# Spreading the first chunk's decays with one single-pass product over 128 stacked rows, and two blocks-of-four of warm-up instead of eleven blocks

## The chip, the cores and the metric

The kernel runs on one core of a Trainium2 chip. The metric is the device time of one execution in microseconds (us). An execution has a span, from its first to its last instruction, and some time around it. The engines are TensorE (PE, its weight loads shown apart as PEld), VectorE (DVE), ScalarE (ACT), GpSimd (POOL) and SyncE (SP), which here only issues DMAs.

## What is computed

A chunked state-space scan (4 batches, 8 heads, 768 positions) is followed by a gated feed-forward layer. Cut to what matters:

```python
for c in range(nc):                                  # chunks of the sequence
    cum = np.cumsum(log_a[:, :, sl], axis=-1)        # log_a = log(clip(a, 1e-6, 1))
    L = np.exp(cum[:, :, :, None] - cum[:, :, None, :]) * causal
    M = np.einsum('bhin,bhjn->bhij', Cc, Bc) * L     # scores times decays
    y[:, :, sl] = einsum(M, xc) + einsum(Cc, state) * exp(cum)
    state = exp(sum(la)) * state + sum(B x, decayed to the chunk's end)
out = (sigmoid(y @ w_gate) * (y @ w_val)) @ w_out    # 3072 tokens, 256 -> 1536 -> 256
```

The kernel never takes a logarithm: the decays L are running products of `a`, made by a multiplying scan.

## The kernel before

The sequence is cut into six chunks of 128 positions, each worked as two halves of 64 (`L2`). The feed-forward layer of a chunk follows once its scan is done, so TensorE has a long, dense middle, and a start in which the first chunk must go through the scan before there is anything to multiply with the weights. The first chunk is worked in four units, one for each batch (class `FirstUnit`), in the order 0, 3, 1, 2.

A planner (`run`) emits every instruction in an order that is fixed by a table of numbers (`DUES`); each engine then executes its own list strictly in that order and waits where a semaphore tells it to. So an early step of an engine that waits for a DMA holds everything behind it on that engine.

What the change touches is the path from the raw `a` to the decays of the first chunk:

- `a0` is the first chunk's `a`, 64 rows (`R2`; half of the chunk, batch, head) of 64 positions, loaded by SP's first DMA.
- `ac` is `a0` clipped, with its first column set to zero (DVE).
- `apart` holds, for each of the 64 rows, its values in the block of 64 columns that belongs to its head, and zeros elsewhere: `ac` times `head2`, a 0/1 selector (DVE). Its lower 64 partitions are filled with zeros by POOL.
- `of_unit[:, b]` is a 0/1 matrix that picks batch b's rows, and repeats them over the 64 partitions of each half. The product of it with `apart` (PE, `spread`, L741, tile `pa`, 128x512, in float32) puts each row's `a` on all partitions that need it.
- The DVE scan at L744 turns `pa` into the decays `dec` (tile `ab`). There are four such products and four such scans, one for each unit.
- Before all that TensorE multiplies a tile of zeros (`warm`, L237): eleven blocks of 128 columns in three instructions, `WARM = (4, 4, 3)`.

Around this path, in the same lists, stand `products` (the transposes `pt` of B and C, L756 and L757, and the score products `pcb`, L691), `result` (DVE's `weigh` L695, which multiplies scores and decays into the tile `m`; then TensorE's L706 and L716), and `split_w`, which cuts a block of weights (tile `wr`) into parts in five steps: DVE L482, ACT L488, DVE L490, ACT L495, POOL L497. The first of them is the split of the first gate block; in DVE's list its step L482 stands ahead of the first scan.

Two waits of DVE's and PE's lists are not plain from the code. The banks of PSUM for `pt`, `pa` and the small product `pp` are three, used in turn: the third `pa` waits for the first scan to read the first `pa`, the fourth for the second scan. And the first `m` waits for the third scan, which stands just ahead of it on DVE.

Of the kernel before, what the change touches and what calls it, by code (L numbers as in the profile page):

```python
# [8 lines left out]
F32 = mybir.dt.float32  # L9
F32R = mybir.dt.float32r  # L10
# [3 lines left out]
ALU = mybir.AluOpType  # L14
# [121 lines left out]
}  # L136
WARM = (4, 4, 3)
PE0 = 5.6


# [40 lines left out]
def tile_ssd_then_gated_ffn(  # L181
# [11 lines left out]
    nc = tc.nc  # L193
    NB, H, S, D = x.shape
# [3 lines left out]
    P = 128  # L198
    L = 128
    L2 = L // 2  # L200
# [14 lines left out]
    const = ctx.enter_context(tc.tile_pool(name="const", bufs=1))  # L215
    ld = ctx.enter_context(tc.tile_pool(name="ld", bufs=2))
    wk = ctx.enter_context(tc.tile_pool(name="wk", bufs=2))
    hp = ctx.enter_context(tc.tile_pool(name="hp", bufs=1))
# [16 lines left out]
    warm = ps_y.tile([P, 512], F32, tag="py", name="warm")  # L235
    for r in WARM:
        nc.tensor.matmul(  # L237
# [3 lines left out]
    eye = const.tile([P, P], F32, name="eye")  # L241
    nc.gpsimd.memset(eye, 0.0)
    nc.gpsimd.affine_select(
        out=eye, in_=eye, compare_op=ALU.not_equal, fill=1.0, base=0, pattern=[[-1, P]], channel_multiplier=1
# [9 lines left out]
    eye2 = hp.tile([P, L2], F32, tag="h7", name="eye2")  # L254
# [7 lines left out]
    R2 = 2 * NB * H  # L262
    low = slice(NB * H, R2)
    of_b2 = const.tile([P, NB, 2], F32, name="of_b")
    nc.vector.tensor_reduce(
        of_b2, eye[:, :R2].rearrange("p (o b h) -> p b o h", o=2, b=NB), axis=mybir.AxisListType.X, op=ALU.add
    )
    head2 = const.tile([R2, H], F32, name="head")
    nc.vector.tensor_reduce(
        head2, eye[:R2, :R2].rearrange("p (k h) -> p h k", h=H), axis=mybir.AxisListType.X, op=ALU.add  # L270
    )
    of_unit = hp.tile([P, NB, P], F32, tag="h8", name="of_unit")
    nc.vector.tensor_copy(
        of_unit.rearrange("p b (o l) -> p b o l", o=2),
        of_b2.rearrange("p b (o l) -> p b o l", l=1).broadcast_to([P, NB, 2, L2]),
# [957 lines left out]
    def last_proj(j):  # L1233
# [42 lines left out]
    a_z = dr.tile([2 * NCH, NB * H, L2], F32, name="a_z")  # L1276
    a_p = dr.tile([NB, H, S], F32, name="a_p")
    w_s = dr.tile([NF, P, 2 * 4 * P], F32, name="w_s")
    apart = hp.tile([P, H, L2], F32, tag="h2", name="apart")
    nc.gpsimd.memset(apart[R2:], 0.0)  # L1280
    a0 = hp.tile([R2, L2], F32, tag="h0", name="a0")
    av = a.rearrange("b h s -> (b h) s")
    nc.sync.dma_start(a0, av[:, :L].rearrange("k (o l) -> o k l", o=2))
    az, ap = (hp.tile([NB * H, S], F32, tag=f"h{10 - i}", name=f"a{i}") for i in range(2))
    nc.scalar.activation(table, table, AF.Sigmoid)
    ac = hp.tile([R2, L2], F32, tag="h11", name="ac")
    nc.vector.tensor_scalar(out=ac, in0=a0, scalar1=1e-6, scalar2=1.0, op0=ALU.max, op1=ALU.min)
    nc.vector.memset(ac[:, :1], 0.0)
    nc.vector.tensor_tensor(
        out=apart[:R2], in0=ac.rearrange("p (o l) -> p o l", o=1).broadcast_to([R2, H, L2]),  # L1290
        in1=head2.rearrange("p (h o) -> p h o", o=1).broadcast_to([R2, H, L2]), op=ALU.mult,
    )
    chunks = "p (c l) -> p c l"

# [187 lines left out]
```

## Time and profile before

| | us |
|---|---|
| median of 3 runs (345.7 to 346.11) | 345.91 |
| the profiled execution, whole | 345.54 |
| its span | 343.7 |

| engine | busy us | share of the span | instructions |
|---|---|---|---|
| PE | 337.9 | 98% | 3144 |
| PEld | 261.7 | 76% | 3144 |
| DVE | 220.2 | 64% | 377 |
| POOL | 180.0 | 52% | 181 |
| ACT | 150.2 | 44% | 277 |

The chain that ended last is made of PE for 98% of the span. A float32 matrix product appears as two matmul records, a float32r one as a single record. Ends of matmuls are modelled in this profile, so of TensorE's steps it is the start of the next weight load or matmul that tells how long one took.

### The profile page before, as it was taken

How to read it: one execution, taken by the hardware profiler on the slowest of the kernel's cores; microseconds unless marked ns; L12 is line 12 of the kernel's file. 1: busy time of each engine (PE TensorE's matmuls, PEld its weight loads, DVE VectorE, ACT ScalarE, POOL GpSimd, SP SyncE). 2: the span in 40 equal slices, each digit the busy share in tenths (PEclk: the TensorE clock that was granted, in tenths of full speed). 3: DMA queues.
4: the chain of work that ended last, by engine and by line, in shares of the span. 5: the costliest groups of instructions: out<-in, count | busy, mean ns of one | idle time of the engine just before them, and what ended most of it. 6: DMA issues, size and time to landing. Idle time of an engine off the chain costs nothing.

```text
span 343.7 us, 7948 instructions
## 1 busy us (share of the span) xinstructions
PE 337.9 (98%) x3144; PEld 261.7 (76%) x3144; DVE 220.2 (64%) x377; ACT 150.2 (44%) x277; POOL 180.0 (52%) x181
## 2 busy tenths in 40 slices
PE   8899999999999999999999999999999999999996
PEld 3474587457888888888888888888888888888885
DVE  5889978956879872456666954566064646856221
ACT  4476987124744230136411513361047557645300
POOL 4646265431646434566774545489427885355500
PEclk9999999999999999999999999999999999999999
DMA  6996899871674376476543621108123733220032
GB/s 107 180 352 209 256 272 146 162 132 35 94 159 62 90 109 159 97 139 89 145 100 102 85 76 21 63 3 297 72 36 91 240 89 110 110 61 2 0 58 67
DMA packets 100247, 40.16 MB, mean 117 GB/s; under 512 B 88754, under 2 KB 91826, under 8 KB 99570
## 3 DMA queue, kind: packets, MB, share of 16 engines
q1 hardware_dynamic: 97906, 39.39, 49.3%
q10 hardware_dynamic: 2304, 0.26, 0.5%
q8 instruction: 25, 0.41, 0.5%
q14 instruction: 12, 0.10, 0.1%
HBM read 30.00 MB, written 9.63 MB: 115 GB/s over the span
## 4 chain that ended last, share of the span: by engine, by line
PE 98%; DVE 1%; ACT 0%; issue 0%
PE pg L981 17%; PE pv L981 17%; PE ux L1121 6%; PE acc L1121 6%; PE po L1017 5%; PE po L1013 5%; PE po L1019 5%; PE po L1018 5%; PE acc L1224 5%; PE uz L1121 5%; PE pg L972 2%; PE pv L972 2%; PE po L1251 2%; PE pcb L706 2%; PE pcb L691 2%; PE pcb L647 2%
## 5 line engine op out<-in xcount | busy, mean ns | idle before, releaser
L981 PE MATMUL pg<-xh,w 128*128 128x512 f32 x168 | 59.0, 392 | 0.0
L981 PE MATMUL pv<-xh,w 128*128 128x512 f32 x168 | 58.9, 391 | 0.0
L927 POOL TENSOR_TENSOR h<-g,h 128x512 fp32r<-128x512 f32 x27 | 38.3, 1420 | 24.4 <-ACT h L925 17.2
L921 DVE TENSOR_TENSOR g<-pv,g 128x512 f32<-128x512 f32 x38 | 26.1, 688 | 30.1 <-PE pv L981 29.1
L903 ACT ACTIVATE g<-pg 128x512 f32<-128x512 f32 x47 | 28.0, 596 | 39.4 <-PE pg L981 37.2
L981 PEld LDWEIGHTS pg<-xh,w 128*128 128x128 f32 x168 | 31.5, 188 | 6.7
L981 PEld LDWEIGHTS pv<-xh,w 128*128 128x128 f32 x168 | 31.5, 188 | 6.6
L497 POOL TENSOR_TENSOR wr<-wr 128x512 int32<-128x512 int32 x18 | 20.5, 1143 | 26.8 <-ACT wr L495 13.0
L981 PE MATMUL pg<-xl,w 128*128 128x512 f32 x84 | 32.7, 389 | 0.0
L981 PE MATMUL pv<-xl,w 128*128 128x512 f32 x84 | 32.7, 389 | 0.0
L1017 PE MATMUL po<-h,w 128*128 128x512 f32 x76 | 30.8, 405 | 0.0
L1019 PE MATMUL po<-h,w 128*128 128x512 f32 x76 | 29.6, 390 | 0.0
L1018 PE MATMUL po<-h,w 128*128 128x512 f32 x76 | 29.6, 389 | 0.0
L577 DVE TENSOR_TENSOR_SCAN ab<-ab,delta 128x512 f32<-128x512 f32 x20 | 28.1, 1424 | 0.0
L925 ACT CAST h<-g 128x512 fp32r<-128x512 f32 x26 | 16.0, 619 | 24.2 <-DVE g L921 24.0
L1048 POOL TENSOR_TENSOR c<-c,c 128x512 f32<-128x512 f32 x13 | 17.2, 1326 | 17.9 <-ACT c L1176 9.2
L1048 POOL TENSOR_TENSOR h<-c,h 128x512 fp32r<-128x512 f32 x16 | 21.0, 1323 | 9.4 <-ACT h L1200 9.3
L1048 POOL TENSOR_TENSOR sw<-sw 128x128 f32<-128x128 f32 x36 | 18.9, 535 | 11.2 <-DVE sw L1048 10.2
L1028 DVE STREAM_TRANSPOSE o<-po 128x256 f32<-128x256 f32 x16 | 6.3, 430 | 21.2 <-PE po L1019 19.2
L1200 ACT CAST h<-c 128x512 fp32r<-128x512 f32 x24 | 14.9, 619 | 10.7 <-POOL c L1048 7.1
L981 PEld LDWEIGHTS pv<-xl,w 128*128 128x128 f32 x84 | 15.8, 188 | 3.2
L981 PEld LDWEIGHTS pg<-xl,w 128*128 128x128 f32 x84 | 15.8, 188 | 3.2
(197 smaller groups left out, 733.2 us busy)
## 6 DMA issues: line engine op xcount, KB each, us to landing
w_s<-sp SPq DMA_DIRECT2D x12, 512.0 KB
s<-w_s SPq DMA_DIRECT2D x12, 512.0 KB
ab<-a_z SPq DMA_DIRECT2D x10, 512.0 KB
wr<-in_moe_w_gate_dram SPq DMA_DIRECT2D x6, 512.0 KB
wr<-in_moe_w_val_dram SPq DMA_DIRECT2D x6, 512.0 KB
wr<-in_moe_w_out_dram SPq DMA_DIRECT2D x6, 512.0 KB
xn<-in_x_dram SPq DMA_DIRECT2D x5, 512.0 KB
out_dram<-o SPq DMA_DIRECT2D x144, 16.0 KB
```

The source lines that it names most:

```text
L497: nc.gpsimd.tensor_tensor(out=lw.bitcast(I32), in0=hw.bitcast(I32), in1=lw.bitcast(I32), op=ALU.add)
L577: nc.vector.tensor_tensor_scan(out=t, data0=t, data1=delta.rearrange("p h l -> p (h l)"), initial=0.0, op0=ALU.mult, op1=ALU.add,)
L903: nc.scalar.activation(gs[k, f], pm, AF.Sigmoid)
L921: nc.vector.tensor_tensor(out=g, in0=pm, in1=g, op=ALU.mult)
L927: engines[eng].tensor_tensor(out=hl, in0=g, in1=hh.bitcast(F32), op=ALU.subtract)
L981: nc.tensor.matmul(pm, w[:, part, kt, fs], xx[:, kt], start=(i == 0), stop=(i == 3 * NK - 1))
L1013: nc.tensor.matmul(acc, whole[NF + f // 2][:, f % 2, ms], hs[k, f], start=start, stop=stop)
L1017: nc.tensor.matmul(acc, hi, hh, start=start, stop=False)
L1018: nc.tensor.matmul(acc, hi, hl, start=False, stop=False)
L1019: nc.tensor.matmul(acc, lo, hh, start=False, stop=stop)
L1048: engines[eng].tensor_tensor(out=out, in0=in0, in1=in1, op=op)
L1121: nc.tensor.matmul(out, a[i], b[j], start=start and n == 0, stop=n == 2, skip_group_check=True)
```

## The change

The products that spread the decays run in float32r, a rounded form of float32, in one pass instead of several. So that little is lost, each value is split into its rounded form and the rest, and both stand in the same product: rows 0 to 63 of `ah` are the rounded `ac`, rows 64 to 127 hold `ac` minus its rounded form, and the selectors `of_unit` and `head2` repeat for the lower 64 rows. For that `a0` is loaded twice, into partitions 0 to 63 by SP's queue and into 64 to 127 by ACT's queue; `ac`, `apart` and `head2` have 128 partitions; POOL's fill with zeros falls away; DVE gets two small steps more, a cast and a subtraction. The warm-up loses its third instruction, three blocks. The table of numbers is the same.

```diff
-WARM = (4, 4, 3)
+WARM = (4, 4)
...
-        of_b2, eye[:, :R2].rearrange("p (o b h) -> p b o h", o=2, b=NB), axis=mybir.AxisListType.X, op=ALU.add
+        of_b2, eye2.rearrange("p (o b h) -> p b o h", o=2, b=NB), axis=mybir.AxisListType.X, op=ALU.add
...
-    head2 = const.tile([R2, H], F32, name="head")
-    nc.vector.tensor_reduce(
-        head2, eye[:R2, :R2].rearrange("p (k h) -> p h k", h=H), axis=mybir.AxisListType.X, op=ALU.add
-    )
-    of_unit = hp.tile([P, NB, P], F32, tag="h8", name="of_unit")
+    head2 = const.tile([P, H], F32, name="head")
+    nc.vector.tensor_reduce(head2, eye2.rearrange("p (k h) -> p h k", h=H), axis=mybir.AxisListType.X, op=ALU.add)
+    of_unit = hp.tile([P, NB, P], F32R, tag="h8", name="of_unit")
...
-    apart = hp.tile([P, H, L2], F32, tag="h2", name="apart")
-    nc.gpsimd.memset(apart[R2:], 0.0)
-    a0 = hp.tile([R2, L2], F32, tag="h0", name="a0")
+    apart = hp.tile([P, H, L2], F32R, tag="h2", name="apart")
+    a0 = hp.tile([P, L2], F32, tag="h0", name="a0")
     av = a.rearrange("b h s -> (b h) s")
-    nc.sync.dma_start(a0, av[:, :L].rearrange("k (o l) -> o k l", o=2))
+    for r, eng in enumerate((nc.sync, nc.scalar)):
+        eng.dma_start(a0[r * R2 : (r + 1) * R2], av[:, :L].rearrange("k (o l) -> o k l", o=2))
...
-    ac = hp.tile([R2, L2], F32, tag="h11", name="ac")
+    ac = hp.tile([P, L2], F32, tag="h11", name="ac")
...
+    ah = wk.tile([P, L2], F32R, tag="sp", name="ah", bufs=1)
+    nc.vector.tensor_copy(ah, ac)
+    nc.vector.tensor_tensor(out=ah[R2:], in0=ac[R2:], in1=ah[R2:].bitcast(F32), op=ALU.subtract)
     nc.vector.tensor_tensor(
-        out=apart[:R2], in0=ac.rearrange("p (o l) -> p o l", o=1).broadcast_to([R2, H, L2]),
-        in1=head2.rearrange("p (h o) -> p h o", o=1).broadcast_to([R2, H, L2]), op=ALU.mult,
+        out=apart, in0=ah.bitcast(F32).rearrange("p (o l) -> p o l", o=1).broadcast_to([P, H, L2]),
+        in1=head2.rearrange("p (h o) -> p h o", o=1).broadcast_to([P, H, L2]), op=ALU.mult,
     )
```

On TensorE the list begins like this before, where `pt` are transposes, `pa` the spreading products, `pp` a small product for the state's decays and `pcb` the scores (a float32 product is one row here):

```order
L237 MATMUL warm<-warm_sb 128x512 x2
L237 MATMUL warm<-warm_sb 128x384
L756 MATMUL pt_141<-eye,bn_127 128x128
L757 MATMUL pt_141<-eye,cq_129 128x128
L741 MATMUL pa_146<-apart,of_unit 128x512
L871 MATMUL pp_154<-apb,of_row 128x256
L741 MATMUL pa_162<-apart,of_unit 128x512
L741 MATMUL pa_167<-apart,of_unit 128x512
```

and like this in the changed kernel:

```order
L237 MATMUL warm<-warm_sb 128x512 x2
L754 MATMUL pt_143<-eye,bn_129 128x128
L755 MATMUL pt_143<-eye,cq_131 128x128
L739 MATMUL pa_148<-apart,of_unit 128x512
L869 MATMUL pp_156<-apb,of_row 128x256
L739 MATMUL pa_164<-apart,of_unit 128x512
L739 MATMUL pa_169<-apart,of_unit 128x512
```

Nothing is moved; one row is gone, and line numbers are two lower.

On DVE the list from the clipping of `a` to the first `m` stands like this before, where `wr` is the first block of gate weights and `ab` the decays:

```order
L1287 TENSOR_SCALAR ac<-a_118 64x64
L1288 MEMSET ac 64x1
L1289 TENSOR_TENSOR apart<-ac,head 64x512
L859 SCALAR_TENSOR_TENSOR ap_139<-at_137,warm_sb 32x64
L482 TENSOR_SCALAR wr_131<-wr_131 128x512
L744 SCALAR_TENSOR_TENSOR ab_158<-pa_146,delta 128x512
L490 TENSOR_SCALAR wr_131<-wt_160 128x512
L744 SCALAR_TENSOR_TENSOR ab_158<-pa_162,delta 128x512
L744 SCALAR_TENSOR_TENSOR ab_158<-pa_167,delta 128x512
L695 TENSOR_TENSOR m_202<-pcb_179,ab_158 128x512
```

and like this in the changed kernel:

```order
L1285 TENSOR_SCALAR ac<-a_116 128x64
L1286 MEMSET ac 128x1
L1288 CAST ah<-ac 128x64
L1289 TENSOR_TENSOR ah<-ac,ah 64x64
L1290 TENSOR_TENSOR apart<-ah,head 128x512
L857 SCALAR_TENSOR_TENSOR ap_141<-at_139,warm_sb 32x64
L480 TENSOR_SCALAR wr_133<-wr_133 128x512
L742 SCALAR_TENSOR_TENSOR ab_160<-pa_148,delta 128x512
L488 TENSOR_SCALAR wr_133<-wt_162 128x512
L742 SCALAR_TENSOR_TENSOR ab_160<-pa_164,delta 128x512
L742 SCALAR_TENSOR_TENSOR ab_160<-pa_169,delta 128x512
```

Two rows came in ahead of `apart`; the step on the weights still stands ahead of the first scan.

## Rows read from the trace of the kernel before

**Rows 1.** Busy time by stage: us, busy us (instructions) by engine, clock, DMA share, GB/s

```profile
6.00:10.00 4.00, 4.00 (x27) 1.58 (x25) 2.97 (x4) 2.41 (x7) 1.59 (x4) 1.00 1.00 105
10.00:18.60 8.60, 7.08 (x237) 4.45 (x221) 7.33 (x16) 5.21 (x19) 4.44 (x10) 1.00 0.98 231
18.60:42.40 23.80, 23.80 (x132) 13.53 (x132) 21.49 (x42) 17.36 (x33) 10.97 (x11) 1.00 0.85 267
```

**Rows 2.** The chain that ended last, its start: start us, us, what

```profile
1.09 5.04 PE warm L237 x6
...
6.36 0.86 PE pa L741 x2
7.21 0.62 PE pp L871 x2
7.84 1.91 PE pa L741 x4
...
10.53 0.88 PE pa L741 x2
11.40 0.68 DVE m L695
...
12.22 0.48 PE pcb L691 x16
...
13.72 0.49 PE pcb L691 x16
```

**Rows 3.** Timeline of DVE: start us, us, line, operation, out<-in, [idle before <-what ended it]

```profile
3.24 0.23 DVE L1287 TENSOR_SCALAR ac<-a 64x64 f32<-64x64 f32 x1 [0.26 <-DMA a<-in_a_dram]
...
3.63 0.68 DVE L1289 TENSOR_TENSOR apart<-ac,head 64x512 f32<-64x512 f32 x1
...
6.89 0.43 DVE L482 TENSOR_SCALAR wr<-wr 128x512 f32<-128x512 f32 x1 [1.98 <-DMA wr<-in_moe_w_gate_dram]
7.25 1.22 DVE L744 TENSOR_TENSOR_SCAN ab<-pa,delta 128x512 f32<-128x512 f32 x1
8.39 0.40 DVE L490 TENSOR_SCALAR wr<-wt 128x512 uint32<-128x512 uint32 x1
8.93 2.34 DVE L744 TENSOR_TENSOR_SCAN ab<-pa,delta 128x512 f32<-128x512 f32 x2
11.38 0.69 DVE L695 TENSOR_TENSOR m<-pcb,ab 128x512 f32<-128x512 f32 x1
...
13.44 0.21 DVE L724 TENSOR_TENSOR sm<-py,mask 128x64 f32<-128x64 f32 x1
...
17.22 0.42 DVE L490 TENSOR_SCALAR wr<-wt 128x512 uint32<-128x512 uint32 x1
17.55 0.22 DVE L724 TENSOR_TENSOR mr<-mm,mask 128x64 f32<-128x64 f32 x1
```

**Rows 4.** Timeline of TensorE's weight loads, columns as in rows 3

```profile
5.31 0.23 PEld L756 LDWEIGHTS pt<-eye,bn 128*128 128x128 f32 x1 [0.30 <-issue]
5.95 0.17 PEld L757 LDWEIGHTS pt<-eye,cq 128*128 128x128 f32 x1 [0.41 <-issue]
...
8.53 0.39 PEld L741 LDWEIGHTS pa<-apart,of_unit 128*128 128x128 f32 x2 [0.47 <-DVE ab L744]
```

**Rows 5.** The chain again, its first group of float32r products

```profile
42.36 1.39 PE pg L981 x6
```

**Rows 6.** Timeline of SP's DMA queue, its first issue, columns as in rows 3

```profile
0.75 0.70 SPq L1283 DMA_DIRECT2D a<-in_a_dram  x1
```

**Rows 7.** DMA queues between 3.0 and 3.4 us: the line of all packets

```profile
DMA packets 676, 0.04 MB, mean 106 GB/s; under 512 B 676, under 2 KB 676, under 8 KB 676
```

**Rows 8.** Timeline of ACT, its first step after the table of sigmoids

```profile
6.44 0.27 ACT L763 COPY bct<-pt 128x128 f32<-128x128 f32 x1 [4.20 <-PE pt L757]
```

**Rows 9.** Timeline of DVE and PE at 41 us: a part of x is made and used

```profile
41.19 0.68 DVE L890 TENSOR_TENSOR xl<-xw,xh 128x512 fp32r<-128x512 f32 x1
...
42.12 0.48 PE L981 MATMUL pg<-xh,w 128*128 128x512 f32 x1
```

## The prediction, written before the changed kernel ran

> **What bounds the kernel now.** First the busy time by stage [rows 1]. From 18.6 to 42.4 us PE is busy in all of its 23.8 us, and the chain stays on PE for 98% of the span. So whatever brings TensorE's work forward at 18.6 us brings the end forward, as long as nothing else becomes late; and what the change touches lies ahead of that. From 6 to 10 us PE reads 4.0 of 4.0 us busy, which looks like the bound. From 10 to 18.6 us DVE has 7.33 of 8.6 us and PE 7.08.
>
> Next the chain itself [rows 2]. It names PE from 1.09 to 11.40 us: the warm-up, then all four spreading products, and only then DVE's first `m`. Read alone it promises much: the products take 0.86, 1.91 (two) and 0.88 us, 3.65 in all.
>
> Then the same stretch from DVE's side [rows 3], where the matter is decided. DVE sat idle for 1.98 us until 6.89 us, and what ended it was the DMA of the first weight block, not a product. The weight step L482 stands ahead of the first scan in DVE's list, before and after. The first scan starts at 7.25 us, 0.36 us after L482: two steps of DVE that wait for nothing follow each other so (L490 at 17.22, the next at 17.55, 0.33). The first product ended at 7.21 by the chain [rows 2]. So two things let the first scan go within 0.04 us of each other, and the change makes only one of them earlier. From there to the first `m` DVE has its own four steps to do: they are the path, and PE runs beside them.
>
> **The change part by part.**
>
> Warm-up: the third instruction (384 columns) goes. Its start shows as the weight load of what follows it, 5.31 us, and the next is at 5.95 [rows 4]: 0.64 us for 384 columns in float32, which a record of two halves makes 1.28 us for the whole instruction. So TensorE is free at 5.95 - 1.28 = 4.67 us.
>
> Spreading products: the 0.86 us of a 128x512 float32 product at 2.4 GHz become one pass; six float32r products of that size take 1.39 us later on [rows 5], 0.23 each. At half the clock it would be 0.46.
>
> The new input of the first product: DVE starts `ac` at 3.24 us, when `a` lands [rows 3]. The cast and the subtraction on 64 columns are not in the trace; the 128x64 step that is takes 0.21 us [rows 3], and with the 0.05 us that a step waits for the one before it I take 0.25 each, 0.5 in all; bounds 0.1 (two steps like the smallest gaps) and 0.9 (two like the 0.43 of a 128x512 step). `apart` moves from 3.63 to 4.13 us, takes 0.68 as before (512 columns on twice the partitions), and ends at 4.8, in the bounds 4.4 to 5.2. POOL's fill, which it waited beside, is gone. The cover for all of it is the time until 7.2 us, when the first scan could go at the earliest: the first product would end by 4.9 + 0.46 + 0.2 (a matmul's way out) = 5.6 us at the slow clock, 1.6 us ahead. If that cover were gone, the 0.5 us would show in full.
>
> The second load of `a`: ACT issues it; SP's takes 0.70 us [rows 6], and ACT has nothing to do until 6.44 us, when the first transposes are done [rows 8]. On the DMA engines it adds 64 packets, four to an engine. Between 3.0 and 3.4 us 676 packets of mostly a quarter of that size went through 16 engines, 9.5 ns each [rows 7]: 0.04 us, and 0.15 if time goes by bytes. That much later everything behind it lands, the first weight block too. I take 0.05. The rule in the Trainium skill (Trainium Kernel Development and Optimization, Key Constraints) is that DMAs issued from different queues share the same 16 DMA engines, so the second queue saves issue time alone; by it the addition stays in the sum as I have it.
>
> Now the path. The first scan starts at 7.25 us and ends at 8.47, as before. L490 follows at 8.39. The second scan started at 8.93 us, 0.54 after L490 [rows 3], where 0.33 is the distance without a wait: it waited for the second product, at 7.84 us and behind `pp` on PE's list [rows 2]. In the changed kernel that product is done before 7.3 us at either clock. Gain 0.54 - 0.33 = 0.21 us. The third product waits for the first scan, 8.53 us before [rows 4]; at 0.23 to 0.46 us it ends by 9.2, and the third scan can start right behind the second at 9.9. So the two scans of 2.34 us run without a break, as they did, and the first `m`, which waits for the third scan, moves from 11.38 to 11.17. The fourth product waits for the second scan and has over a microsecond. Everything after hangs on `m`: the score products at 12.22 us waited for it [rows 2], and the rest of the stage goes back and forth between DVE and PE, with steps that the change does not touch.
>
> Sum: 0.21 - 0.05 = 0.16 us less at 18.6 us. Bounds: 0.06 (DMA at 0.15) and 0.21. The 3.65 us of products and the 1.28 of warm-up are worth nothing more, since DVE waits for the weights either way. Does the rest keep the gain? Where TensorE's stage after 42 us begins, `xl` ends at 41.87 us and is used by the group that starts at 42.12 [rows 9]: 0.25 us of room, so a gain of 0.16 fits, one of 0.5 would not without DVE's coming along. Against the profiled execution of 345.54 us the sum gives 345.38. The median of the runs shown is 0.37 us higher; taken off that it is 345.91 - 0.16 = **345.75 us**. A measurement of this kernel can tell about 0.2% (0.69 us) from no change, so this counts as no change.
>
> **The rivals.**
>
> *The clock stays at 1.2 GHz, slower than before.* In the trace a 384-column instruction takes 1.28 us until 5.95 us and a 512-column one 0.86 us after: TensorE went from 1.2 to 2.4 GHz there, having worked without a break since 1.09 us. In the changed kernel it works on end only to 4.67 us; then come transposes when C lands, a product of 0.46 us, `pp`, another product, and between about 7.2 us and the first scan's end at 8.47 nothing at all; from there to 12 us it has some 1.5 us of work. If the clock does not rise, or falls again, nothing is lost up to 11.2 us, since the products are 1.5 us ahead or more. The loss begins where PE is on the path: from 12.22 to the end of the second score products at 14.21 us [rows 2], 1.99 us which would be doubled at most. Behind that point DVE and ACT set much of the pace again, and I take the clock as risen by 18.6 us, where TensorE's work becomes dense. Price 1.99 less the 0.16: +1.8 us, 347.7; from 346.4 (only the last part slow) to 349 (slow until 20 us). What speaks against it: between 14 and 18.6 us TensorE already had pauses, 7.08 of 8.6 us busy from 10 us on [rows 1], and kept its clock. The Trainium skill (TensorE: Matmul & The Clock Gate, Part 1) has it that the slow state is the default and that activity is what releases the clock; that is this rival's mechanism, and the trace agrees with its first half by the row at 5.95 us. It decides from about 12 us on: a clock that rises before that costs nothing.
>
> *More gain than the sum.* If in some runs of the kernel before the clock rises later than in the profiled one, its products and `pp` would have been on the path there (3.65 us of them at double length), while the changed kernel would not feel it. The spread of the runs shown, 345.54 to 346.11, leaves 0.4 us for that; with the 0.16 the time would be 345.3. And if DVE did not wait for the weights, the products would give up to 2 us, 343.9; against that stands the 1.98 us with the DMA's name on it [rows 3].
>
> *The gain is taken back.* The weights that land later by 0.05 to 0.15 us hold each next stage, and the 0.25 us of room is used up: 345.9, inside the same band.
>
> **How the numbers follow.** The forecast and the rival that takes it back lie within 0.2% (345.22 to 346.60) and have 0.45 and 0.15. The clock has 0.25: 0.23 beyond the band, 0.02 in it. More gain has 0.15, most of it beyond 345.22 only if several things add up. Faster by over 0.2%: 0.15; within: 0.62; slower: 0.23. The range goes from 345.0 to 347.7: it leaves out some 0.07 below, and 0.12 above, the upper half of the clock's case.
>
> **What would show it.** Right: the second scan starts 0.33 to 0.36 us behind L490 and the first `m` at about 11.2 us, DVE's step on the weights still waits for its DMA until about 6.9 us, and the chain names DVE from 7 to 11 us where it named PE. The products show as four records of one pass. Wrong: a float32 transpose or score product that takes twice as long after 12 us than before (the clock); a weight DMA that ends much before or after 6.9 us; the first scan waiting for PE, which would mean that `apart` or the second load of `a` is late by over 1.6 us; or a shift at 18.6 us that differs from the one at the end by more than 0.2 us, which would mean that the later stages are not simply PE's.

## The result, and the profile after

The changed kernel takes 347.92 us (median of 6 runs, 347.55 to 350.13) against 345.62 us for the kernel before (6 runs, 345.21 to 346.11) on the same chip. The ratio is 1.0080, 95% interval 1.0062 to 1.0098: slower by 2.3 us. The forecast was 345.75 us, no change; the time is that of the rival in which TensorE's clock falls, and lies 0.2 us above the range. All that follows is read from the profiled execution of 347.95 us, span 346.2 us, against 345.54 us and 343.7 us before.

First the busy time by stage, columns as in [rows 1] (length, then busy us of PE, PEld, DVE, ACT, POOL, then the granted clock), of the changed kernel:

```profile
4.00:6.00 2.00, 1.42 (x5) 0.44 (x3) 1.50 (x6) 0.23 (x2) 0.40 (x2) 1.00 0.96 202
6.00:8.00 2.00, 1.13 (x3) 0.48 (x3) 0.49 (x2) 0.70 (x5) 0.40 (x1) 0.96 0.95 148
8.00:10.00 2.00, 0.88 (x9) 0.45 (x17) 2.00 (x3) 1.47 (x3) 0.98 (x3) 0.50 1.02 97
10.00:12.00 2.00, 1.93 (x21) 1.07 (x21) 1.90 (x3) 0.77 (x4) 1.79 (x3) 0.50 1.01 138
...
20.00:22.00 2.00, 2.00 (x52) 1.48 (x34) 1.30 (x3) 0.42 (x2) 1.04 (x1) 0.63 1.04 294
22.00:24.00 2.00, 2.00 (x68) 1.63 (x68) 0.99 (x5) 1.10 (x3) 0.00 (x0) 1.00 0.94 320
```

The granted clock is 0.96 from 6 to 8 us, 0.50 (1.2 GHz) from 8 to 20, and 0.63 from 20 to 22. A stretch at 0.50 in part gives the moments: it fell at 8.00 - 2.00 x 0.04 / 0.50 = 7.84 us and rose at 20.00 + 2.00 x 0.37 / 0.50 = 21.5 us. That the column reads 1.00 before its first change does not mean full speed from the start (see the last section). In the kernel before the column reads 1.00 all through, and PE is busy in 6.00 of the 6 us from 4 to 10, where the changed kernel has 1.42 + 1.13 + 0.88 = 3.43 us. By the mean clock of each run, five of the six runs lost it so (0.975 to 0.98); one reads 1.00 and took 348.87 us.

Then DVE's timeline, the answer to [rows 3] (line numbers are smaller by two, so L480 is L482 of before):

```profile
3.80 0.25 DVE L1285 TENSOR_SCALAR ac<-a 128x64 f32<-128x64 f32 x1 [0.82 <-DMA a<-in_a_dram]
...
4.21 0.20 DVE L1288 CAST ah<-ac 128x64 fp32r<-128x64 f32 x1
4.44 0.22 DVE L1289 TENSOR_TENSOR ah<-ac,ah 64x64 fp32r<-64x64 f32 x1
4.70 0.69 DVE L1290 TENSOR_TENSOR apart<-ah,head 128x512 fp32r<-128x512 f32 x1
...
7.51 0.43 DVE L480 TENSOR_SCALAR wr<-wr 128x512 f32<-128x512 f32 x1 [1.80 <-DMA wr<-in_moe_w_gate_dram]
7.85 1.22 DVE L742 TENSOR_TENSOR_SCAN ab<-pa,delta 128x512 f32<-128x512 f32 x1
8.98 0.40 DVE L488 TENSOR_SCALAR wr<-wt 128x512 uint32<-128x512 uint32 x1
9.30 2.33 DVE L742 TENSOR_TENSOR_SCAN ab<-pa,delta 128x512 f32<-128x512 f32 x2
11.73 0.69 DVE L693 TENSOR_TENSOR m<-pcb,ab 128x512 f32<-128x512 f32 x1
...
15.59 1.29 DVE L693 TENSOR_TENSOR m<-pcb,ab 128x512 f32<-128x512 f32 x2 [1.14 <-PE pcb L689]
```

The first scan still stands behind the weights' DMA, which now landed at 7.51 us and not at 6.89; the second scan starts 0.32 us behind L488; the first `m` comes at 11.73 us, 0.35 later than in [rows 3].

Last the chain, the answer to [rows 2], where the clock is paid for:

```profile
12.57 0.74 PE pcb L689 x16
...
14.83 0.66 PE pcb L689 x16
...
18.62 1.15 PE py L287 x4
...
20.68 1.48 PE pgv L960 x4
...
24.22 2.79 PE pgv L960 x12
```

In the kernel before the same pieces read:

```profile
17.03 0.71 PE py L289 x4
...
18.60 1.07 PE pgv L962 x4
...
21.73 2.79 PE pgv L962 x12
```

The scores `pcb` take 0.74 and 0.66 us where [rows 2] has 0.48 and 0.49, `py` 1.15 for 0.71. The shift grows from 0.35 us at the first `m`, which is the later weights and not the clock, to 2.08 at the first `pgv` (20.68 against 18.60) and 2.49 at the twelve `pgv` (24.22 against 21.73). It is 2.50 at the next group (27.02 against 24.52) and 346.2 - 343.7 = 2.5 us in the span: all is lost before 24 us and nothing is given back.

### The profile page after: what moved, and what is told of

Its sections match the earlier page's. It is cut to its first block, busy times and chain, and to the rows that moved or that the text cites. A ratio compares the mean times of both kernels' runs of the same rounds, so it can differ in the third digit from the quotient of the medians.

```text
span 346.2 us, 7938 instructions
## 1 busy us (share of the span) xinstructions
PE 338.9 (98%) x3138; PEld 263.1 (76%) x3138; DVE 220.2 (64%) x379; ACT 150.6 (43%) x277; POOL 178.4 (52%) x180
## 4 chain that ended last, share of the span: by engine, by line
PE 95%; DVE 2%; DMA 1%; SPq 1%; issue 0%; DVEq 0%
PE pg L979 17%; PE pv L979 17%; PE ux L1119 6%; PE acc L1119 6%; PE po L1015 5%; PE po L1011 5%; PE po L1017 5%; PE po L1016 5%; PE acc L1222 5%; PE uz L1119 5%; PE pv L970 2%; PE pg L970 2%; PE po L1249 2%; PE pcb L689 2%; PE pcb L704 2%; PE pcb L645 2%
## 5 line engine op out<-in xcount | busy, mean ns | idle before, releaser
L495 POOL TENSOR_TENSOR wr<-wr 128x512 int32<-128x512 int32 x18 | 20.5, 1144 | 28.3 <-ACT wr L493 22.2
```

The costliest lines, as they stand in the source:

```text
L495: nc.gpsimd.tensor_tensor(out=lw.bitcast(I32), in0=hw.bitcast(I32), in1=lw.bitcast(I32), op=ALU.add)
```

## The experiments

Ten kernels, in four questions.

### Is it the shorter warm-up, or the second load?

The kernel before with the shorter warm-up alone:

```diff
-WARM = (4, 4, 3)
+WARM = (4, 4)
```

> The kernel before with only the warm-up cut to two instructions (WARM = (4, 4)); products, loads and DVE steps as before. Theory A (the fall of the clock comes from the spreading products having become a quarter as long, so that TensorE stands idle between them): TensorE is still dense from 5.4 to 12 us with its float32 products, the clock reads 1.00 from 8 us on, and the time is within 0.6 us of the kernel before (345.0 to 346.2), since DVE waits for the weights until 6.9 us either way. Theory B (the shorter warm-up alone is the cause): granted clock 0.50 somewhere between 6 and 20 us, and 347 to 348.

Measured: 345.54 us, ratio 1.0000 (0.9990 to 1.0009), clock 0.998 to 1.00 in ten runs. The second scan stands 0.32 us behind L490 and the first `m` at 11.27 us. So the second scan loses its wait with the shorter warm-up alone. In the time the shorter warm-up costs nothing, and gives nothing either.

The changed kernel with the long warm-up:

```diff
-WARM = (4, 4)
+WARM = (4, 4, 3)
```

> The changed kernel with the old warm-up (WARM = (4, 4, 3)). Theory A: TensorE still idles between 7.3 and 9.1 us and most of 9.4 to 12.5, the clock falls to 0.50 there as in the changed kernel, and the time is 347.3 to 348.2. Theory B: clock 1.00 throughout, first m at 11.7 us, time 345.7 to 346.2.

Measured: 347.32 us, ratio 1.0056 (1.0036 to 1.0075), clock 0.98 to 0.985; the granted clock is 0.63 from 8 to 10 us, then 0.50 until 22 us:

```profile
8.00:10.00 2.00, 0.88 (x9) 0.45 (x17) 2.00 (x3) 1.47 (x3) 0.98 (x3) 0.63 1.04 98
```

The longer warm-up doesn't hold the clock.

The kernel before with the second load of `a`, into partitions that nothing reads:

```diff
-    a0 = hp.tile([R2, L2], F32, tag="h0", name="a0")
+    a0 = hp.tile([P, L2], F32, tag="h0", name="a0")
-    nc.sync.dma_start(a0, av[:, :L].rearrange("k (o l) -> o k l", o=2))
+    for r, eng in enumerate((nc.sync, nc.scalar)):
+        eng.dma_start(a0[r * R2 : (r + 1) * R2], av[:, :L].rearrange("k (o l) -> o k l", o=2))
```

> The kernel before with only the second load of a added, issued from ACT's queue into partitions 64 to 127 that nobody reads. Expected: the first weight block lands at 7.4 to 7.6 us instead of 6.9, the first m at 11.9 to 12.0, the clock stays at 1.00, and the time is 0.4 to 0.7 us above the kernel before (346.0 to 346.3). If the second load explains all of the change's loss: 347.5 or more. If it is free, as the prediction had it: within 0.1.

Measured: 345.49 us, ratio 1.0001 (0.9991 to 1.0010). The loss that was expected did not come; it is the case in which the load is free. On DVE:

```profile
3.77 0.26 DVE L1288 TENSOR_SCALAR ac<-a 64x64 f32<-64x64 f32 x1 [0.79 <-DMA a<-in_a_dram]
...
7.10 0.43 DVE L482 TENSOR_SCALAR wr<-wr 128x512 f32<-128x512 f32 x1 [1.93 <-DMA wr<-in_moe_w_gate_dram]
```

`a` does land 0.53 us later than in [rows 3]. The weights land 0.21 us later, but in the kernel with the short warm-up, which has no second load, they land at 7.04 us too. The time feels none of it.

### Do the passes hold the clock?

Two kernels that change the number of passes, and in the second the rounding that comes with one pass. The first is the changed kernel with each product done four times over:

```diff
-            nc.tensor.matmul(pa, of_unit[:, b], apart.rearrange("p h l -> p (h l)"), start=True, stop=True)
+            for _ in range(4):
+                nc.tensor.matmul(pa, of_unit[:, b], apart.rearrange("p h l -> p (h l)"), start=True, stop=True)
```

> The changed kernel, but each of the four spreading products is done four times over into the same bank (the last one stands; what is computed is the same), so that TensorE has as many passes there as in the kernel before; the second load, the two new DVE steps and the short warm-up stay. Theory A, the clock: TensorE falls to 1.2 GHz at about 8 us because the one-pass products leave it nearly idle from 7 to 9 us. Then the granted clock is 1.00 in every stretch from 8 to 22 us, the score products of unit 0's second half take about 0.49 us again and not 0.66, and the time is 345.2 to 346.2 us, level with the kernel before. Theory B, that something else of the edit costs the time (the load, the new steps, weights that land later): 347.3 us or more, whatever the clock does.

Measured: 345.52 us, ratio 1.0013 (0.9996 to 1.0030). One of its stages (PE is busy in all of 6 to 12 us), its first three products on PE, and its chain at 12 and 21 us:

```profile
8.00:10.00 2.00, 2.00 (x9) 1.42 (x8) 1.82 (x3) 1.18 (x3) 1.28 (x3) 1.00 1.01 95
```

```profile
5.54 1.94 PE L740 MATMUL pa<-apart,of_unit 128*128 128x512 f32 x4
...
8.03 2.11 PE L740 MATMUL pa<-apart,of_unit 128*128 128x512 f32 x8
```

```profile
12.54 0.48 PE pcb L689 x16
...
21.87 2.80 PE pgv L961 x12
```

Once it has risen the clock holds, `pcb` is back at 0.48 us, and the loss is gone (to within 0.3%), with twelve passes more than the changed kernel and with its short warm-up, its load and its new DVE steps all in place. Two things differ in this trace besides the passes. The clock rose only at about 7.2 us: the first four passes took 1.94 us, the eight from 8.03 us on 2.11. And the weights landed at 7.21 us, not 7.51; here the second scan then waited for a product, so that the first `m` comes at 11.70 us all the same, 0.32 later than in [rows 3], of which 0.14 is left at the twelve `pgv` (21.87 against 21.73). The other ten runs have no trace, but all read a mean clock of 0.999 or 1.00. One of the eleven runs took 348.79 us at a mean clock of 1.00; nothing in its record says why.

The second is the kernel before with the one-pass products alone:

```diff
-    of_unit = hp.tile([P, NB, P], F32, tag="h8", name="of_unit")
+    of_unit = hp.tile([P, NB, P], F32R, tag="h8", name="of_unit")
-    apart = hp.tile([P, H, L2], F32, tag="h2", name="apart")
-    nc.gpsimd.memset(apart[R2:], 0.0)
+    apart = hp.tile([P, H, L2], F32R, tag="h2", name="apart")
+    nc.gpsimd.memset(apart[R2:].bitcast(F32), 0.0)
```

> The kernel before with only its four spreading products in one float32r pass; the full warm-up, one load of a, no new DVE step. The decays' low part is left out, so they are spread with the rounded value alone. Theory A: the granted clock falls to 0.50 between 7 and 9 us and is back by 22 us, and the time is 347.0 to 348.3 us. Theory B: without the load and the new steps nothing is lost, clock 1.00 throughout, 345.3 to 345.9 us.

Measured: 348.27 us, ratio 1.0076 (1.0060 to 1.0092), clock 0.98 to 0.985; the profiled execution, at 347.02 us, is the fastest of the four. Its stages and its chain:

```profile
6.00:8.00 2.00, 1.70 (x7) 0.74 (x5) 1.00 (x2) 1.43 (x5) 0.00 (x0) 1.00 1.00 103
8.00:10.00 2.00, 1.38 (x19) 0.69 (x19) 2.00 (x4) 0.98 (x3) 1.47 (x4) 0.84 1.03 97
```

```profile
12.07 0.73 PE pcb L691 x16
...
23.18 2.80 PE pgv L962 x12
```

The full warm-up, one load, no new step, weights that land at 7.00 us, a first `m` at 11.24 us, and still the clock falls, at 10.00 - 2.00 x 0.16 / 0.50 = 9.36 us, and reads 0.50 in the next stretches. So the one pass is enough for the loss, and more passes are enough to cure it. That settles the cause as far as the parts of this change go.

A third kernel on the same question is the changed one with products of zeros (128 columns, float32) put behind each spreading product (these go in the order of batches 3, 1, 0, 2, so there are 1, 7, 4 and 2 of them, each of two records):

```diff
+            for _ in range({3: 1, 1: 7, 0: 4, 2: 2}[b]):
+                nc.tensor.matmul(warm[:, :P], warm_sb, warm_sb, start=True, stop=True)
```

> The changed kernel with products of zeros (128 columns, float32) behind the four spreading products, 1, 7, 4 and 2 of them, into the warm-up's unused bank, so that TensorE is about as busy between 6 and 12 us as before. Theory A: clock 1.00 from 8 us on, first m at 11.7 us (0.35 later than before: weights 0.6 later, second scan 0.2 closer), time 345.8 to 346.2. If the loss is the late weights and steps of DVE and not the clock: 347.5 to 348, whatever the clock does.

Measured: 348.58 us, ratio 1.0077 (1.0047 to 1.0107). On the weight loads of TensorE and on DVE:

```profile
7.69 3.15 PEld L741 LDWEIGHTS warm<-warm_sb 128*128 128x128 f32 x14
...
10.87 1.09 PEld L741 LDWEIGHTS warm<-warm_sb 128*128 128x128 f32 x8
```

```profile
11.30 1.22 DVE L744 TENSOR_TENSOR_SCAN ab<-pa,delta 128x512 f32<-128x512 f32 x1 [1.27 <-PE pa L739]
```

In this execution the fourteen loads behind the second product took 3.15 us, 0.22 each, where the eight behind the next one took 0.14 each: TensorE was still slow until about 10.5 us. So the fill itself got onto the path, the third scan waited 1.27 us for it: the fill was sized for full speed. The clock also fell in this execution, but later: it reads 0.71 from 20 to 22 us and 0.50 from 22 to 24, behind two microseconds from 18 on in which TensorE had 0.68 us of work. The time that was expected with the clock held, 345.8 to 346.2 us, was missed, and the run does not tell the two cases apart.

### Would the products be worth something if DVE did not wait for the weights?

The forecast said that a scan held by the weights makes the products worthless, and that they would be worth up to 2 us otherwise. In the kernel before, with the short warm-up, the first weight block's step L482 (and ACT's that uses it) was put behind the third scan, and its later steps on DVE and ACT behind the first `m`; GpSimd's list stays. In DVE's list:

```diff
-L482 TENSOR_SCALAR wr
 L744 SCALAR_TENSOR_TENSOR ab
-L490 TENSOR_SCALAR wr
 L744 SCALAR_TENSOR_TENSOR ab
 L744 SCALAR_TENSOR_TENSOR ab
+L482 TENSOR_SCALAR wr
 L695 TENSOR_TENSOR m
+L490 TENSOR_SCALAR wr
```

> The kernel before with the short warm-up, and with the first weight block's step on DVE (L482) behind the third scan in DVE's list and not ahead of the first one; its later steps stand behind the first m. The prediction said that the products are worth something as soon as DVE does not wait for the weights. If so, the first scan starts when the first product is done (about 6.0 us, before 7.38 in the same kernel without this edit), the first m comes at about 10.3 us (before 11.27), and the time is 344.5 to 345.1 us. If what comes after m waits for something else (x, the transposes, the later weights), the first m is earlier but from 18 us on nothing is: 345.3 to 345.8 us.

and the same in the changed kernel with products done four times over:

> The changed kernel with each spreading product done four times over, and with the first weight block's step behind the third scan as in the run beside it. If the clock stays at 1.00: first scan at about 5.9 us, first m at about 10.0 us, 344.3 to 345.1 us if the rest keeps it, 345.3 to 345.9 us if x or the weights set the rest. If the clock falls again, as in the changed kernel: 347 us or more.

Measured: 349.60 us, ratio 1.0116 (1.0096 to 1.0136), and 349.70 us, ratio 1.0123 (1.0108 to 1.0138). Neither expectation had that cause; the second one had such a time only if the clock fell as in the changed kernel. The first `m` did come early, at 10.87 us in the first of them, but on GpSimd:

```profile
13.09 1.04 POOL L502 TENSOR_TENSOR wr<-wr 128x512 int32<-128x512 int32 x1 [4.07 <-ACT wr L500]
14.08 0.78 POOL L803 TENSOR_TENSOR bd<-bn,ab 128x128 f32<-128x128 f32 x2
```

GpSimd's weight step kept its place in its list and now waited 4.07 us for ACT's; the `bd` of the first output stand behind it and came at 14.08 us, where the kernel before has them at 11.35. TensorE then had 0.86 us of work in the 2 us from 12, and lost its clock besides, at 16.00 - 2.00 x 0.15 / 0.50 = 15.4 us by the 0.85 of that stretch. With the products done four times over it is the same, 0.86 us of work from 12 to 14 us and a clock of 0.74 from 14 to 16: the pause lies behind the products.

So the edit was made smaller: each of DVE's two steps only one scan later, and no other list touched. DVE's list:

```diff
-L482 TENSOR_SCALAR wr
 L744 SCALAR_TENSOR_TENSOR ab
-L490 TENSOR_SCALAR wr
+L482 TENSOR_SCALAR wr
 L744 SCALAR_TENSOR_TENSOR ab
+L490 TENSOR_SCALAR wr
 L744 SCALAR_TENSOR_TENSOR ab
```

> The kernel before with the short warm-up, and with the first weight block's two DVE steps each one scan later: L482 behind the first scan, L490 behind the second; no other engine's list is touched. In the run with all of them behind the third scan, GpSimd's weight step stood ahead of its steps for the first output and held them until 14.1 us; here it should start at about 10 us as in the kernel before. If DVE's wait for the weights was what made the products worthless: first scan at about 6.6 us (before 7.25), second at 8.3 (before 8.93), first m at about 10.9 us (before 11.38), and 0.3 to 0.5 us less in all, 344.9 to 345.2 us with the kernel before at 345.4. If the first output waits for something else (the transposes, x): the first m is earlier but from 18.6 us on nothing is, 345.3 to 345.6 us. If TensorE's clock falls in the longer pauses: 347 us or more.

Measured: 345.63 us over eleven runs, ratio 1.0000 (0.9987 to 1.0014). Its profiled execution is one of the two fastest, at 344.84 us:

```profile
6.52 1.22 DVE L755 TENSOR_TENSOR_SCAN ab<-pa,delta 128x512 f32<-128x512 f32 x1 [1.62 <-PE pa L752]
7.66 0.40 DVE L489 TENSOR_SCALAR wr<-wr 128x512 f32<-128x512 f32 x1
8.20 1.22 DVE L755 TENSOR_TENSOR_SCAN ab<-pa,delta 128x512 f32<-128x512 f32 x1
...
11.02 0.69 DVE L706 TENSOR_TENSOR m<-pcb,ab 128x512 f32<-128x512 f32 x1
```

```profile
21.17 2.79 PE pgv L975 x12
```

There the first scan waits for PE and no longer for the weights. The kernel that it is to be held against is the one with the short warm-up alone, whose profiled execution took 345.13 us:

```profile
11.27 0.69 DVE L695 TENSOR_TENSOR m<-pcb,ab 128x512 f32<-128x512 f32 x1
```

```profile
21.42 2.80 PE pgv L962 x12
```

Against it `m` and the twelve `pgv` come 0.25 us earlier, and the span is 0.2 shorter. The runs, 344.80 to 346.49 us here and 344.93 to 345.75 there, each with a ratio of 1.0000, show no such gain, and only one run of each left a trace. So a gain of some tenths is not shown, and what would take it back is open.

### Is it the pause behind the late weights that loses the clock?

In the changed kernel TensorE had nothing to do between 7.57 and 9.12 us, since its third product waits for the first scan and that for the weights. The same swap in the changed kernel, products done once, takes that pause away:

> The changed kernel, products done once, with the same swap of DVE's steps: its first scan need not wait for the weights. First scan at about 5.9 us, second at about 7.6, first m at 10.3 to 10.8 us. Theory A, the clock: TensorE is just as idle as in the changed kernel, the granted clock falls to 0.50 between 7 and 10 us and is back at 20 to 22 us, 347.0 to 348.2 us in spite of the earlier m. If the fall came from the late weights (PE idle only because the scans were held): clock 1.00, 344.5 to 345.3 us.

Measured: 347.69 us, ratio 1.0061 (1.0048 to 1.0075). The profiled execution:

```profile
6.00:8.00 2.00, 1.55 (x12) 0.92 (x20) 1.90 (x3) 1.08 (x5) 0.40 (x1) 0.93 1.07 137
```

```profile
10.46 0.69 DVE L704 TENSOR_TENSOR m<-pcb,ab 128x512 f32<-128x512 f32 x1
```

The first `m` is 1.27 us earlier than in the changed kernel, and the clock falls all the same, at 8.00 - 2.00 x 0.07 / 0.50 = 7.7 us, while TensorE is at work:

```profile
7.07 0.74 PE L750 MATMUL pa<-apart,of_unit 128*128 128x512 f32 x2
```

Three of the four runs read a mean clock of 0.98; the fourth reads 0.999 and is no faster, 347.89 us. The late weights are not the cause, and mending DVE's order does not bring the changed kernel back to the one before. No kernel of these beats the kernel before; one with the swap, one-pass products and a clock that holds was not tried, so what the products are worth then is not shown.

## Why the prediction was wrong

**The chance of the clock.** This is the step that failed: the sum put the products and the warm-up that TensorE loses at nothing, and the rival in which they cost the clock got 0.25. The runs show the clock at 1.2 GHz for 13.7 us in its place, and 2.3 us more where 0.16 less was forecast. It happened in the changed kernel and in each kernel with one pass per product and nothing put beside them. The argument against it was that from 10 to 18.6 us TensorE had 7.08 of 8.6 us of work [rows 1] and kept its clock. But from 6 to 10 us the changed kernel has only 1.13 + 0.88 = 2.01 us of work in 4, where [rows 1] show 4.00, so that stretch is no measure for this one. The terms were there to be added up: 4 x (0.86 - 0.23) = 2.5 us of products and 1.28 us of warm-up fewer, out of work that had no break at all. I read those 3.8 us only for what they are worth on the path, which is nothing, and did not ask what else they did. Of the two, the products are what counts: the 1.28 us taken out of the kernel before cost nothing, and put back into the changed kernel they did not hold the clock.

**Where in that rival.** The prediction pointed to the pause from 7.2 us to the end of the first scan. In the changed kernel the clock fell at 7.84 us, 0.27 us after the last product before that pause had ended; and with the pause gone it fell at 7.7 us, during work, as it did at 9.36 us in the kernel with one pass alone:

```profile
9.04 0.51 PE L691 MATMUL pcb<-bct 32*64 32x128 f32 x16
```

So it is not that pause by itself; what is left is the thinner work from 4 us on, in which these are the pieces on PE in the changed kernel:

```profile
5.36 0.33 PE L755 MATMUL pt<-eye,cq 128*128 128x128 f32 x1 [0.53 <-DMA cq<-in_C_dram]
5.45 0.50 PE L739 MATMUL pa<-apart,of_unit 128*128 128x512 f32 x1
6.45 0.69 PE L869 MATMUL pp<-apb,of_row 32*128 32x256 f32 x2 [0.50 <-POOL apb L862]
7.07 0.50 PE L739 MATMUL pa<-apart,of_unit 128*128 128x512 f32 x1
9.12 0.79 PE L739 MATMUL pa<-apart,of_unit 128*128 128x512 f32 x1 [1.55 <-DVE ab L742]
```

The first two products, 0.50 us in the record, ran at 2.4 GHz and the third, 0.79, at 1.2: the clock had come up and fell again. Which of the rows decides when it falls, the profile does not show: the kernel with the short warm-up alone had PE busy in 1.72 and 1.35 us of the two stretches from 6 to 10 us and kept its clock, the one with one pass alone had 1.70 and 1.38 and lost it. These stretches are not alike, since the clock rose at 4.92 us in the first and at 5.95 in the second.

**Its price.** 1.8 us was forecast and the medians differ by 2.3. That this is near is partly luck. The price was one stretch, 12.22 to 14.21 us at half speed, and the clock taken as risen by 18.6 us. At the end of that stretch stands the second pair of `m`, which waited 1.14 us for `pcb` in the changed kernel (15.59 us) and 0.58 in the kernel before:

```profile
14.23 1.29 DVE L695 TENSOR_TENSOR m<-pcb,ab 128x512 f32<-128x512 f32 x2 [0.58 <-PE pcb L691]
```

The shift is 15.59 - 14.23 = 1.36 us there, and 0.35 of it was there at the first `m`; so the stretch cost 1.0 us and not 1.99. The clock rose only some 3 us later than assumed, and work of TensorE was on the path in between: the shift grew by another 0.72 us to the first `pgv` and by 0.41 from there to the twelve. The upper end of the range, 347.7, was cut at the price of the one stretch.

**The first scan behind the weights.** Right as a mechanism [rows 3]: the same DMA ends the same wait, and the products and the warm-up bring nothing. The 0.62 us by which that DMA landed later were not foreseen. They are not all the change's: with the second load the step on the weights starts at 7.01 to 7.51 us in five traces, without it at 6.89 to 7.04 in three.

**The second scan.** Right: 0.32 us behind L488, where 0.33 was worked out, though the shorter warm-up alone brings the same; the 0.21 us went into the later weights.

**The second load.** Mis-sized: 0.05 us, bounded by 0.15, was taken from the packets' own time [rows 7]. `ac`, which waits for `a`, starts at 3.58 to 3.95 us in the seven traces with it and at 3.12 to 3.29 in the five without. The issue on ACT's queue, which was taken as SP's 0.70 us, is 0.43 us longer:

```profile
0.75 1.13 ACTq L1281 DMA_DIRECT2D a<-in_a_dram  x1
```

SP's next load took 0.64 us to issue too, where it had 0.41, and the weights behind it were issued at 2.81 us and not at 2.58. The Trainium skill (Trainium Kernel Development and Optimization, Key Constraints) was cited for the rule that the queues share the 16 DMA engines and a second one saves issue time alone. It does not say what two issues side by side cost, 1.13 and 0.64 us here; no run has both loads on one queue, so what the second queue saved is not shown. In the time it is nothing, as the load alone and the products done four times over both show.

**The new steps on DVE.** Right: from `ac` to `apart` it is 0.90 us where it was 0.39 [rows 3], 0.51 more for 0.5 forecast, and `apart` ends at 5.39 us, 2.1 us ahead of the weights, though behind the bound of 5.2 because `a` came later.

**From 18.6 us to the end.** Right only from 24 us on: the shift at the first `pgv`, 2.08 us, and that at the end, 2.5, differ by more than the 0.2 us that were named as a sign, since the clock was still low. What is lost at 24 us is lost at the end, to within 0.02 us; the room of 0.25 us at 42 us [rows 9] does not matter to a delay.

**The sum.** With the clock held by products done four times over, the edit costs 0.13% (-0.04% to 0.30%), most of it inside the band that was called no change. The 0.16 us of gain was not seen there, and could not be in full: with four passes the second scan waits for its product again.

## What to carry to other kernels

Work that is worth nothing on the path can still be what keeps an engine's clock up. Before taking passes from TensorE in a stretch where another engine sets the pace, add up its busy time there before and after the edit, and price everything that follows at half speed; if that price is larger than the gain, the saving wants a place where TensorE is the bound. And when a step is moved on one engine, look at what stands behind its successors in the other engines' lists.

## What the runs showed of the hardware

In the changed kernel the clock fell 0.27 us after TensorE's last work, with no pause above 0.53 us since TensorE started at 1.09 us; in the kernel with one pass alone (9.36 us) and in the one with the swap (7.7 us) it fell while TensorE was at work. It took until 19.6 to 22.2 us to come back in the four kernels that lost it so, though in the changed kernel PE was busy in 9.46 of the 10 us from 10 to 20.

The granted clock in the table by stage reads 1.00 from the start, also where the rows run at half speed: the weight loads of the warm-up stand 0.85 us apart in every kernel; with the products done four times over the passes are slow until about 7.2 us, and with the zero products the weight loads are until about 10.5 us. The trace records no clock ahead of the first rise, and the table counts that time as 1.00. Its record begins at 5.99 us in the kernel before, 4.43 in the changed kernel, 4.92 with the short warm-up alone, 5.22 with the second load, 7.20 with the products done four times over and 10.60 with the zero products; where weight loads or products stand close to that moment, their pace changes there.

So the first rise differs by several microseconds between executions, also of kernels with the same warm-up. The Trainium skill (TensorE: Matmul & The Clock Gate, Part 1) says that the point of the rise varies from run to run, by 0.5 us either way. That it varies agrees with these records, and 5.99 and 5.22 us with the long warm-up lie 0.8 us apart; 4.43 to 10.60 us with the short one is a much wider spread. A late rise may also be why single runs are slow at a mean clock of 1.00 (348.79 us with the products done four times over, 348.87 in the changed kernel); these left no trace, so it is not shown.
